# Attention and two feed-forward layers in one kernel: a new order of the first loads, six staging buffers, order edges for the weight decoding, and softmax sums in PSUM

## The chip, the cores and the metric

The kernel runs on one core of a Trainium2 chip. The metric is the device time of one launch in microseconds (us), from start to end, all inputs in HBM at the start and the output in HBM at the end. PE is the matrix engine, ACT, DVE and POOL are the three element-wise engines, SP is the queue from which all loads and stores are issued.

## The reference, cut to what matters

Inputs are q, k, v of 2 batches, 8 heads, 576 positions and 64 columns. Two attentions are added: a local one with a band mask, and one over positions averaged in groups of four, whose output is repeated four times. Its result is the x of a gated layer, and that layer's output the x of a layer of four experts.

```
def sm_attn(qq, kk, vv):          # softmax(qq kk^T / 8) vv
...
out_d = sm_attn(q_d, k_d, v_d)    # q_d, k_d, v_d: means over 4 positions
mask = np.abs(pos[:, None] - pos[None, :]) < 4
scores = np.where(mask, scale * q @ k^T, -1e9)
out_local = softmax(scores) @ v
x = np.repeat(out_d, 4, axis=2) + out_local      # then heads side by side: [1152, 512]
h = x @ w_in                                     # [512, 2048]
x = (h / (1 + np.exp(-h))) @ w_out               # [2048, 512]
for e in range(4):
    out += p[:, e:e + 1] * (np.maximum(x @ w1[e], 0) @ w2[e])
```

## The kernel before, in words

**Attention.** The work is cut into 16 jobs (class Job, `plan_jobs`, L470): a job is one batch, one pair of heads and one of two pieces of positions (256 or 320 queries, four or five blocks of 64). Its steps are put at ticks: `load_kq`, `load_vg`, `load_vw` (L251 to L280), `local_scores` (L345), `local_max`, `local_exp`, `local_sum` (L362 to L374), the pooled keys (`pool_kq_first` for jobs 0 to 3, L312, on PE, ACT and DVE; `pool_kq` on POOL for the rest), `down_scores` and `down_max` (L376, L388), `norm` (L396), `trans` (L405, L413 to L423), `values` (L432, L441 to L452) and `split_x` (L454), which writes the job's part of x as a rounded part xh (L457, ACT) and a rest xl (L458, DVE). Scores lie in PSUM tiles of a pool with two buffers (`s_p`), transposes and outputs in one each (`t_p`, `o_p`). The statistics of a job (maxima, sums, reciprocals) lie in a small SBUF tile `j.st`, in every second column.

**Weights.** The gated layer's weights come as 8 units of four pieces, s0 to s31, 512 KB each (`load_raw`, L173). Units 0 and 1 are the first half of `w_in`, units 2 and 3 the first half of `w_out`, units 4 to 7 the second halves. A piece lands in a staging buffer of the pool `stg` (three buffers) and is decoded by `split_raw` (L190): two ACT operations (L201, L202), one on DVE (L203), then the rounded part on ACT (L207) and the rest on POOL (L208). `split_piece` then loads the next piece (`load_piece`). The DVE operation of unit 1 is tied behind the last x of jobs 0 to 2, that of units 2 and 3 behind that of job 3 (`behind_job`); the ACT operations are tied to nothing.

**Products.** The gated layer runs over four chunks of positions (256, 320, 256, 320) and two halves. In the first chunk the first three column groups are started per job by `start_mm` (one piece of unit 0 and the x of one job each). `g1_step` makes h, `g1_evac` its gate (L540 to L547), `g2_step` the second product, whose sum for the first half goes to `acc` (L571). Every product is three matmuls of rounded parts and rests (`mm3`, L521). The experts follow (L664, L725, `outputs`).

**The order.** Each instruction has a priority (`prio`, `at_prio`), and the compiler's list scheduler orders every engine's queue by priority and its own estimate of when data are there; at run time each engine takes its queue strictly in order. `follow` adds an edge that fixes only an order. The names in `FIRST_LOADS` (L120) give the first loads their order on SP's queue. At L804 to L807 `LOAD_AT` and `SPLIT_AT` put the first calls of `load_piece` and `split_piece` at ticks. `shares` (L821) loads the expert shares `dpr`.

Of the kernel before, what the change touches and what calls it, by code (L numbers as in the profile page):

```python
# [42 lines left out]
LOAD_AT = (-27, -13, -10)  # L43
# [18 lines left out]
def attention_moe_kernel(ctx, tc, kqa, kqb, qtl, va, vb, w64, w1d, w2d, dpr, out):  # L62
# [57 lines left out]
    FIRST_LOADS = ("kq0", "kq1", "s0", "s1", "vg0", "vw0", "s2", "kq2", "vg1", "vw1", "s3", "kq3", "vg2", "vw2",  # L120
                   "vg3", "vw3", "s4", "s5", "s6", "kq4", "kq5")
# [25 lines left out]
    last_x = []  # L147
# [25 lines left out]
    def load_raw(u, j):  # L173
        if u < 8:
            t = stg_p.tile([128, 512], I64, tag="stg", name="stg64")
            load(f"s{4 * u + j}", t, w64[u, :, j * 512:(j + 1) * 512])
        else:
            t = stg_p.tile([128, 1024], F32, tag="stg", name="stg")
            o = (u - 8) * UW + j * 1024
            SP.dma_start(out=t, in_=w1d[0, :, o:o + 1024])  # L180
        loaded.append((u, j, t))

    def split_piece():
        u, j, t = loaded.popleft()
        with at_prio(needed(u, j) - LEAD_SPLIT):
            split_raw(u, j, t)
        held[0] -= 1
        load_piece()

    def split_raw(u, j, t):  # L190
        if j == 0:
            unit[u] = slot(u)
        h, l = unit[u]
        if u < 8:
            c = slice(j * 512, (j + 1) * 512)
            v = t.bitcast(I32).rearrange("p (n t) -> p n t", t=2)
            a = d_p.tile([128, 512], F32, tag="dec", name="dec")
            ai = a.bitcast(I32)

            top = t.bitcast(U16).rearrange("p (n t) -> p n t", t=4)[:, :, 1]  # L200
            ACT.activation(out=a, in_=v[:, :, 1].bitcast(F32), func=ACTF.Prelu, scale=2.0 ** -112, alpha=2.0 ** 32)  # L201
            ACT.activation(out=v[:, :, 0], in_=top, func=ACTF.Copy, scale=2.0 ** -13, bias=2.0 ** -14 - 0.5)  # L202
# [4 lines left out]
            ACT.activation(out=h[:, c], in_=a, func=ACTF.Copy)  # L207
            POOL.tensor_tensor(out=l[:, c], in0=a, in1=h[:, c].bitcast(F32), op=ALU.subtract)  # L208
# [54 lines left out]

    def load_vw(j):
        if j.i in (2, 3):
            j.vw = first_p.tile([72, 512], F32, name=f"vw_f{j.i}")
        else:
            j.vw = a2.tile([72, 640], F32, tag="vw", name="vw")
        if j.c == 0:
            load(f"vw{j.i}", j.vw[:, 0:512], va[j.b, j.hp, :, 1024:1536])  # L270
        else:
            SP.dma_start(out=j.vw, in_=vb[j.b, j.hp])

    def load_vg(j):
        if j.c == 0:
# [4 lines left out]
            load(f"vg{j.i}", j.vg, va[j.b, j.hp, :, 0:1024])  # L280
# [92 lines left out]
    def local_sum(j):  # L373
        DVE.tensor_reduce(out=j.st[:, 7:7 + j.nb], in_=j.lo, axis=AX.X, op=ALU.add)  # L374
# [6 lines left out]
    def tail_scores(l):  # L381
# [4 lines left out]
        l.st = a2.tile([128, 20, 2], F32, tag="st", name="st")[:, :, 0]  # L386

    def down_max(j):  # L388
# [65 lines left out]
    def split_x(j):  # L454
        n, hp = j.n, j.hp
        x0 = XOFF[2 * j.b + j.c]
        ACT.activation(out=xh[:, hp, x0:x0 + n], in_=j.xf[:, 0:n], func=ACTF.Copy)  # L457
# [3 lines left out]
        if j.i < 4:  # L461
            behind_job.update({1: i} if j.i < 3 else {2: i, 3: i})
# [358 lines left out]
    def shares():  # L821
        SP.dma_start(out=pr, in_=dpr)
# [169 lines left out]
```

## Time and profile before

| | us |
|---|---|
| three runs | 682.25, 689.22, 687.2 |
| their median | 687.2 |
| the profiled execution, device time | 688.92 |
| its span in the trace | 686.8 |

All times of the trace count from the start of the span. The profiled execution lies 1.7 us above the median; 2.1 us of its time lie around its span. Loads and stores are shown under SPq, where the time is that of issuing, not of the transfer. A row of the timeline merges neighbours of the same kind (x4: four of them) and ends with the idle time of its engine before it and what ended that.

### The profile page before, as it was taken

How to read it: one execution, taken by the hardware profiler on the slowest of the kernel's cores; microseconds unless marked ns; L12 is line 12 of the kernel's file. 1: busy time of each engine (PE TensorE's matmuls, PEld its weight loads, DVE VectorE, ACT ScalarE, POOL GpSimd, SP SyncE). 2: the span in 40 equal slices, each digit the busy share in tenths (PEclk: the TensorE clock that was granted, in tenths of full speed). 3: DMA queues.
4: the chain of work that ended last, by engine and by line, in shares of the span. 5: the costliest groups of instructions: out<-in, count | busy, mean ns of one | idle time of the engine just before them, and what ended most of it. 6: DMA issues, size and time to landing. Idle time of an engine off the chain costs nothing.

```text
span 686.8 us, 13770 instructions
## 1 busy us (share of the span) xinstructions
PE 654.2 (95%) x5516; PEld 637.2 (93%) x5516; DVE 422.4 (61%) x850; ACT 330.1 (48%) x753; POOL 244.2 (36%) x346
## 2 busy tenths in 40 slices
PE   5689879999999999999999999999999999999996
PEld 4568769998999999999999999999999999999995
DVE  3458957655534653675476875558854669755444
ACT  4459766557653642443335643346533355433321
POOL 4434851133330000552265433455422654332210
PEclk9999989999999999999999999999999999999998
DMA  8847652025130300050001320003210020000001
GB/s 235 283 128 228 186 163 71 22 63 185 62 123 2 114 10 1 5 191 20 1 1 63 124 61 2 1 18 107 93 31 1 1 63 1 1 31 23 11 32 46
DMA packets 16928, 48.17 MB, mean 70 GB/s; under 512 B 2976, under 2 KB 4256, under 8 KB 16864
## 3 DMA queue, kind: packets, MB, share of 16 engines
q1 hardware_dynamic: 16864, 47.29, 22.0%
q8 instruction: 43, 0.70, 0.4%
q14 instruction: 21, 0.17, 0.1%
HBM read 44.93 MB, written 2.36 MB: 69 GB/s over the span
## 4 chain that ended last, share of the span: by engine, by line
PE 85%; DMA 6%; DVE 4%; ACT 3%; issue 1%; SPq 0%; ACTq 0%; DVEq 0%
PE mm L521 54%; PE p L725 26%; DMA stg<-in_w_dram 6%; PE s L353 1%; DVE dec L203 1%; PE t L413 1%; ACT dec L201 1%; PE o L445 1%; PE o L441 1%; ACT stg L202 1%; DVE acc L753 1%; DVE gl L547 0%; DVE st L398 0%; PE s L377 0%; SPq L128 0%
## 5 line engine op out<-in xcount | busy, mean ns | idle before, releaser
L521 PE MATMUL mm<-xh,wbuf 128*128 128x256 f32 (+2 forms) x1280 | 266.2, 295 | 1.2 <-ACT xh L457 1.0
L521 PEld LDWEIGHTS mm<-xh,wbuf 128*128 128x128 f32 x1280 | 209.6, 189 | 1.7 <-ACT xh L457 1.3
L521 PE MATMUL mm<-xl,wbuf 128*128 128x256 f32 (+2 forms) x640 | 188.7, 295 | 0.0
L707 POOL TENSOR_TENSOR r<-r 128x128 f32<-128x128 f32 x160 | 93.4, 596 | 183.2 <-ACT r L701 143.8
L710 DVE TENSOR_TENSOR h<-r,h 128x384 fp32r<-128x384 f32 (+1 forms) x128 | 91.7, 719 | 64.6 <-ACT h L709 64.4
L521 PEld LDWEIGHTS mm<-xl,wbuf 128*128 128x128 f32 x640 | 120.7, 189 | 0.1
L709 ACT ACTIVATE h<-r 128x384 fp32r<-128x384 f32 (+1 forms) x128 | 73.2, 577 | 85.2 <-POOL r L707 54.1
L521 PE MATMUL mm<-gh,wbuf 128*128 128x256 f32 (+2 forms) x512 | 105.3, 299 | 3.6 <-DVE gf L541 2.0
L725 PE MATMUL p<-wext,h 128*128 128x256 f32 x672 | 91.5, 279 | 0.0
L521 PEld LDWEIGHTS mm<-gh,wbuf 128*128 128x128 f32 x512 | 83.7, 191 | 4.6 <-ACT acc L571 1.5
L725 PE MATMUL p<-wbuf,h 128*128 128x256 f32 x672 | 84.5, 278 | 0.0
L725 PEld LDWEIGHTS p<-wext,h 128*128 128x128 f32 x672 | 84.4, 188 | 0.0
L725 PEld LDWEIGHTS p<-wbuf,h 128*128 128x128 f32 x672 | 81.2, 188 | 0.0
L521 PE MATMUL mm<-gl,wbuf 128*128 128x256 f32 (+2 forms) x256 | 74.6, 297 | 0.0
L701 ACT ACTIVATE r<-mm 128x512 f32<-128x512 f32 x48 | 28.6, 597 | 75.9 <-PE mm L521 75.5
L707 DVE TENSOR_TENSOR r<-r 128x128 f32<-128x128 f32 x96 | 33.4, 349 | 37.7 <-ACT r L701 33.1
L547 DVE TENSOR_TENSOR gl<-gf,gh 128x256 fp32r<-128x256 f32 (+2 forms) x64 | 38.5, 609 | 17.6 <-ACT gh L546 16.6
L521 PEld LDWEIGHTS mm<-gl,wbuf 128*128 128x128 f32 x256 | 48.9, 191 | 0.1
L541 DVE SCALAR_TENSOR_TENSOR gf<-th,mm 128x256 f32<-128x256 f32 (+2 forms) x64 | 28.6, 450 | 24.6 <-ACT th L540 23.7
L208 POOL TENSOR_TENSOR wbuf<-dec,wbuf 128x512 fp32r<-128x512 f32 x24 | 32.5, 1363 | 28.5 <-DVE gf L541 14.2
L753 DVE SCALAR_TENSOR_TENSOR acc<-p,pr,acc 128x256 f32<-128x256 f32 (+1 forms) x63 | 36.1, 605 | 5.9 <-PE p L725 5.9
L652 POOL TENSOR_TENSOR wext<-kst,wext 128x512 fp32r<-128x512 f32 x8 | 10.7, 1343 | 78.8 <-ACT wext L650 44.6
(130 smaller groups left out, 946.8 us busy)
## 6 DMA issues: line engine op xcount, KB each, us to landing
stg<-in_w_dram SPq DMA_DIRECT2D x32, 512.0 KB
kst<-in_w2d_dram SPq DMA_DIRECT2D x16, 512.0 KB
kst<-in_w1d_dram SPq DMA_DIRECT2D x12, 512.0 KB
kq<-in_kqa_dram SPq DMA_DIRECT2D x7, 419.0 KB
kq<-in_kqb_dram SPq DMA_DIRECT2D x8, 323.0 KB
stg<-in_w1d_dram SPq DMA_DIRECT2D x4, 512.0 KB
vw<-in_vb_dram SPq DMA_DIRECT2D x8, 180.0 KB
out_dram<-acc SPq DMA_DIRECT2D x5, 256.0 KB
```

The costliest lines, as they stand in the source:

```text
L201: ACT.activation(out=a, in_=v[:, :, 1].bitcast(F32), func=ACTF.Prelu, scale=2.0 ** -112, alpha=2.0 ** 32)
L208: POOL.tensor_tensor(out=l[:, c], in0=a, in1=h[:, c].bitcast(F32), op=ALU.subtract)
L521: ins = [PE.matmul(out=ps, lhsT=l, rhs=r, start=(first and i == 0), stop=(last and i == n - 1)) for i, (l, r) in enumerate(pairs)]
L541: DVE.scalar_tensor_tensor(out=gf[:, 0:n], in0=th[:, 0:n], scalar=1.0, in1=ps[:, 0:n], op0=ALU.add, op1=ALU.mult)
L547: latest[DVE] = DVE.tensor_tensor(out=gl[ft][:, 0:n], in0=gf[:, 0:n], in1=gh[ft][:, 0:n].bitcast(F32), op=ALU.subtract)
L652: b = eng.tensor_tensor(out=l[:, r], in0=x, in1=h[:, r].bitcast(F32), op=ALU.subtract)
L701: ACT.activation(out=r[:, 0:4].rearrange("p s t -> p (s t)"), in_=ps[:, 0:512], func=ACTF.Relu)
L707: latest[eng] = eng.tensor_tensor(out=r[:, o], in0=r[:, a], in1=r[:, b], op=op)
L709: ACT.activation(out=h, in_=r[:, part], func=ACTF.Copy)
L710: latest[DVE] = DVE.tensor_tensor(out=l, in0=r[:, part], in1=h.bitcast(F32), op=ALU.subtract)
L725: ins = [PE.matmul(out=ps, lhsT=x, rhs=y, start=(opens and k == 0 and i == 0), stop=(k == 3 and i == n - 1), skip_group_check=True) for i, ...
L753: DVE.scalar_tensor_tensor(out=o, in0=ps, scalar=p, in1=o, op0=ALU.mult, op1=ALU.add)
```

## The change

The first loads have a new order: keys, queries and values of jobs 0 to 3, then the weights. Job 3's keys get a place in `acc`, which is unused until the first `g2_step`, in place of a shared buffer. Six pieces are requested before the first is decoded; of the first 16 pieces those with i % 6 > 2 lie in `acc`, the others in the three staging buffers. Pieces are decoded behind given operations by order edges: s0, s1 behind the normalization of job 0 and s2, s3 behind that of job 1 (both ACT operations behind its ACT scaling, the DVE operation behind its DVE product), s4, s5 behind the x of job 0, s6, s7 behind that of job 2, units 2 and 3 behind that of job 3. The loads for jobs 8 and 9 are tied behind the load of s13, and the load of the expert shares behind the last load of the attention. The sums of the two softmaxes go to unused columns of the job's score tile in PSUM, the statistics tile has one column beside the other.

```
-LOAD_AT = (-27, -13, -10)
+LOAD_AT = (-27, -13, -10, -10, -10, -10)
...
-    FIRST_LOADS = ("kq0", "kq1", "s0", "s1", "vg0", "vw0", "s2", "kq2", "vg1", "vw1", "s3", "kq3", "vg2", "vw2",
-                   "vg3", "vw3", "s4", "s5", "s6", "kq4", "kq5")
+    FIRST_LOADS = ("kq0", "kq1", "vg0", "vw0", "kq2", "vg1", "vw1", "kq3", "vg2", "vw2", "vg3", "vw3",
+                   "s0", "s1", "s2", "s3", "kq4", "s4", "s5", "kq5")
...
     def load_raw(u, j):
         if u < 8:
-            t = stg_p.tile([128, 512], I64, tag="stg", name="stg64")
-            load(f"s{4 * u + j}", t, w64[u, :, j * 512:(j + 1) * 512])
+            i = 4 * u + j
+            if i < 16 and i % 6 > 2:
+                o = 1024 * (i % 6 - 2)
+                t = acc[:, o:o + 1024].bitcast(I64)
+            else:
+                t = stg_p.tile([128, 512], I64, tag="stg", name="stg64")
+            piece_load.append(load(f"s{4 * u + j}", t, w64[u, :, j * 512:(j + 1) * 512]))
...
     def split_piece():
         u, j, t = loaded.popleft()
+        i = 4 * u + j
...
-        load_piece()
+        if i < 10 or 11 < i < 15 or i > 15:
+            load_piece()
...
-            if u in behind_job:
-                follow(i, behind_job[u], "first weights")
+            key = (u, j) if u < 2 else u
+            if key in behind_job:
+                for a in (first, low):
+                    follow(a, behind_job[key][0], "first weights")
+                follow(i, behind_job[key][1], "first weights")
...
     def load_kq(j):
         kw = S + 6 if j.c == 0 else CT[1] + 6
-        if j.i == 2:
+        if j.i == 3:
+            j.kq = acc[:, 0:kw + j.n]
+        elif j.i == 2:
...
+        elif j.i in (8, 9):
+            follow(i, piece_load[j.i + 5], "weights")
...
-        j.st = a2.tile([128, 20, 2], F32, tag="st", name="st")[:, :, 0]
+        j.st = a2.tile([128, 20], F32, tag="st", name="st")
...
-        DVE.tensor_reduce(out=j.st[:, 7:7 + j.nb], in_=j.lo, axis=AX.X, op=ALU.add)
+        DVE.tensor_reduce(out=j.ps[:, 496:496 + j.nb], in_=j.lo, axis=AX.X, op=ALU.add)
...
-                       accum_out=j.st[:, 7 + j.nb:8 + j.nb])
+                       accum_out=j.ps[:, 496 + j.nb:497 + j.nb])
...
     def norm(j):
         nb = j.nb
-        DVE.tensor_scalar(out=j.st[:, 7:8 + nb], in0=j.st[:, 7:8 + nb], scalar1=1e-9, scalar2=None, op0=ALU.add)
-        DVE.reciprocal(out=j.st[:, 13:14 + nb], in_=j.st[:, 7:8 + nb])
+        sums = j.ps[:, 496:497 + nb]
+        DVE.tensor_scalar(out=sums, in0=sums, scalar1=1e-9, scalar2=None, op0=ALU.add)
+        DVE.reciprocal(out=j.st[:, 13:14 + nb], in_=sums)
...
+        if nb and j.i < 2:
+            behind_job.update({(0, 2 * j.i): (a, i), (0, 2 * j.i + 1): (a, i)})
...
     def split_x(j):
...
-        if j.i < 4:
-            behind_job.update({1: i} if j.i < 3 else {2: i, 3: i})
+        for key in {0: ((1, 0), (1, 1)), 2: ((1, 2), (1, 3)), 3: (2, 3)}.get(j.i, ()):
+            behind_job[key] = (a, i)
...
     def shares():
-        SP.dma_start(out=pr, in_=dpr)
+        follow(SP.dma_start(out=pr, in_=dpr), last_load[-1], "shares")
```

## Rows read from the trace of the kernel before

**Rows 1.** The page: PE's busy share in 40 slices of the span, in tenths.

```profile
PE   5689879999999999999999999999999999999996
```

**Rows 2.** Windows: busy us (instructions) per engine, granted clock, DMA share, GB/s.

```profile
0.00:54.60 54.60, 36.52 (x319) 28.15 (x319) 26.42 (x70) 28.71 (x70) 23.38 (x43) 0.97 0.70 211
54.60:91.90 37.30, 33.58 (x404) 30.04 (x403) 33.87 (x73) 31.92 (x87) 27.41 (x38) 0.96 0.69 217
0.00:91.90 91.90, 70.09 (x721) 58.19 (x721) 60.29 (x143) 60.64 (x156) 50.79 (x80) 0.96 0.70 214
91.90:100.40 8.50, 5.81 (x48) 5.46 (x48) 4.24 (x12) 4.66 (x14) 4.17 (x9) 0.71 0.52 159
100.40:140.00 39.60, 39.60 (x447) 35.82 (x446) 24.22 (x70) 22.77 (x70) 4.08 (x12) 0.98 0.15 41
...
0.00:30.00 30.00, 17.10 (x119) 12.89 (x120) 12.26 (x31) 13.81 (x31) 15.73 (x30) 1.00 0.90 273
...
60.00:70.00 10.00, 10.00 (x116) 9.39 (x114) 9.21 (x24) 10.00 (x31) 4.45 (x6) 1.00 0.76 250
```

**Rows 3.** The chain that ended last, in order of time: start us, us, what.

```profile
3.52 10.76 DMA stg<-in_w_dram
...
16.01 8.42 DMA stg<-in_w_dram
...
161.60 147.31 PE mm L521 x1134
```

**Rows 4.** Timeline of ACT, from 14 to 35 us.

```profile
14.30 0.66 ACT L202 ACTIVATE stg<-stg 128x512 int32<-128x512 uint16 x1 [1.25 <-DMA stg<-in_w_dram]
14.86 0.39 ACT L371 ACTIVATE s<-s 128x280 f32<-128x280 f32 x1
...
34.17 0.39 ACT L371 ACTIVATE s<-s 128x280 f32<-128x280 f32 x1
34.84 0.66 ACT L202 ACTIVATE stg<-stg 128x512 int32<-128x512 uint16 x1 [0.28 <-DMA stg<-in_w_dram]
```

**Rows 5.** Timeline: the ends of jobs 2 and 3, and the last piece of unit 3.

```profile
44.20 0.41 DVE L458 TENSOR_TENSOR xl<-o,xh 128x256 fp32r<-128x256 f32 x1
...
54.16 0.42 DVE L458 TENSOR_TENSOR xl<-o,xh 128x256 fp32r<-128x256 f32 x1 [0.23 <-ACT xh L457]
...
90.60 1.28 POOL L208 TENSOR_TENSOR wbuf<-dec,wbuf 128x512 fp32r<-128x512 f32 x1
```

**Rows 6.** Timeline: first scores, job 0's subtraction and weights' product, job 3's keys issued.

```profile
4.08 2.20 PE L353 MATMUL s<-kq 64*64 64x70 f32 x32 [4.08 <-DMA kq<-in_kqa_dram]
...
7.50 0.46 DVE L367 TENSOR_TENSOR s<-s,st 128x280 f32<-128x280 f32 x1
...
18.34 0.37 SPq L128 DMA_DIRECT2D kq<-in_kqa_dram  x1
...
20.11 0.81 DVE L402 TENSOR_TENSOR sm<-s,st 128x280 f32<-128x280 f32 x2
```

**Rows 7.** Groups of ACT, 0 to 91.9 us: busy us, mean ns | idle before.

```profile
L202 ACT ACTIVATE stg<-stg 128x512 int32<-128x512 uint16 x19 | 12.7, 669 | 4.0 <-DMA stg<-in_w_dram 3.9
L201 ACT ACTIVATE dec<-stg 128x512 f32<-128x512 f32 x17 | 11.3, 667 | 11.3 <-DMA stg<-in_w_dram 11.2
L207 ACT ACTIVATE wbuf<-dec 128x512 fp32r<-128x512 f32 x16 | 10.0, 628 | 0.6 <-DVE dec L203 0.6
```

**Rows 8.** Groups of DVE, 0 to 91.9 us, adding 1e-9 to the sums, and the pooled maximum.

```profile
L398 DVE TENSOR_SCALAR st<-st 128x5 f32<-128x5 f32 (+2 forms) x11 | 5.6, 520 | 0.5 <-ACT ed L393 0.4
...
L391 DVE TENSOR_REDUCE st<-s 128x1 f32<-128x144 f32 x11 | 3.3, 299 | 2.5 <-PE s L377 2.5
```

**Rows 9.** Line 398 alone (min/median/max ns), and its longest with POOL's row beside it.

```profile
L398 DVE TENSOR_SCALAR st<-st x18: 154/169/2273, 19.3 to 131.0; 128x5 f32<-128x5 f32 x8, 128x6 f32<-128x6 f32 x8, 128x1 f32<-128x1 f32 x2
...
80.75 2.27 DVE L398 TENSOR_SCALAR st<-st 128x5 f32<-128x5 f32 x1
...
81.72 1.27 POOL L208 TENSOR_TENSOR wbuf<-dec,wbuf 128x512 fp32r<-128x512 f32 x1
```

More of the change, by code (lines that the diff above doesn't have):

```diff
@@ L196, in split_raw @@
             v = t.bitcast(I32).rearrange("p (n t) -> p n t", t=2)
-            a = d_p.tile([128, 512], F32, tag="dec", name="dec")
-            ai = a.bitcast(I32)
+            d = d_p.tile([128, 512], F32, tag="dec", name="dec")
+            ai = d.bitcast(I32)
             top = t.bitcast(U16).rearrange("p (n t) -> p n t", t=4)[:, :, 1]
-            ACT.activation(out=a, in_=v[:, :, 1].bitcast(F32), func=ACTF.Prelu, scale=2.0 ** -112, alpha=2.0 ** 32)
-            ACT.activation(out=v[:, :, 0], in_=top, func=ACTF.Copy, scale=2.0 ** -13, bias=2.0 ** -14 - 0.5)
+            first = ACT.activation(out=d, in_=v[:, :, 1].bitcast(F32), func=ACTF.Prelu, scale=2.0 ** -112, alpha=2.0 ** 32)
+            low = ACT.activation(out=v[:, :, 0], in_=top, func=ACTF.Copy, scale=2.0 ** -13, bias=2.0 ** -14 - 0.5)
             i = DVE.scalar_tensor_tensor(out=ai, in0=ai, scalar=3, in1=v[:, :, 0],
                                          op0=ALU.logical_shift_left, op1=ALU.bitwise_or)
-            if u in behind_job:
-                follow(i, behind_job[u], "first weights")
-            ACT.activation(out=h[:, c], in_=a, func=ACTF.Copy)
-            POOL.tensor_tensor(out=l[:, c], in0=a, in1=h[:, c].bitcast(F32), op=ALU.subtract)
+            key = (u, j) if u < 2 else u
[3 more added lines that the diff above has]
+                follow(i, behind_job[key][1], "first weights")
+            ACT.activation(out=h[:, c], in_=d, func=ACTF.Copy)
+            POOL.tensor_tensor(out=l[:, c], in0=d, in1=h[:, c].bitcast(F32), op=ALU.subtract)
         else:
@@ L279, in load_vg @@
                 j.vg = ac.tile([128, 256, 4], F32, tag="vg", name="vg")[0:72]
-            load(f"vg{j.i}", j.vg, va[j.b, j.hp, :, 0:1024])
+            i = load(f"vg{j.i}", j.vg, va[j.b, j.hp, :, 0:1024])
+            if j.i == 8:
+                follow(i, piece_load[13], "weights")
     def load_tail(l):
@@ L385, in tail_scores @@
                       rhs=kd[l.b, hp], start=True, stop=True, tile_position=(0, 32 * hp))
-        l.st = a2.tile([128, 20, 2], F32, tag="st", name="st")[:, :, 0]
+        l.st = a2.tile([128, 20], F32, tag="st", name="st")
     def down_max(j):
@@ L393, in down_max @@
         ACT.activation(out=j.ed, in_=pd, func=ACTF.Exp, scale=SC_D, bias=j.st[:, 6:7],
-                       accum_out=j.st[:, 7 + j.nb:8 + j.nb])
+                       accum_out=j.ps[:, 496 + j.nb:497 + j.nb])
     def norm(j):
         nb = j.nb
-        DVE.tensor_scalar(out=j.st[:, 7:8 + nb], in0=j.st[:, 7:8 + nb], scalar1=1e-9, scalar2=None, op0=ALU.add)
-        DVE.reciprocal(out=j.st[:, 13:14 + nb], in_=j.st[:, 7:8 + nb])
+        sums = j.ps[:, 496:497 + nb]
+        DVE.tensor_scalar(out=sums, in0=sums, scalar1=1e-9, scalar2=None, op0=ALU.add)
+        DVE.reciprocal(out=j.st[:, 13:14 + nb], in_=sums)
         if nb:
             j.sm = a2.tile([128, nb, WIN], F32, tag="sm", name="sm")
-            DVE.tensor_tensor(out=j.sm, in0=j.lo, in1=j.st[:, 13:13 + nb].unsqueeze(2).to_broadcast([128, nb, WIN]), op=ALU.mult)
-        ACT.activation(out=j.ed, in_=j.ed, func=ACTF.Copy, scale=j.st[:, 13 + nb:14 + nb])
+            i = DVE.tensor_tensor(out=j.sm, in0=j.lo, in1=j.st[:, 13:13 + nb].unsqueeze(2).to_broadcast([128, nb, WIN]), op=ALU.mult)
+        a = ACT.activation(out=j.ed, in_=j.ed, func=ACTF.Copy, scale=j.st[:, 13 + nb:14 + nb])
+        if nb and j.i < 2:
+            behind_job.update({(0, 2 * j.i): (a, i), (0, 2 * j.i + 1): (a, i)})
     def trans(j):
@@ L456, in split_x @@
         x0 = XOFF[2 * j.b + j.c]
-        ACT.activation(out=xh[:, hp, x0:x0 + n], in_=j.xf[:, 0:n], func=ACTF.Copy)
+        a = ACT.activation(out=xh[:, hp, x0:x0 + n], in_=j.xf[:, 0:n], func=ACTF.Copy)
         i = DVE.tensor_tensor(out=xl[:, hp, x0:x0 + n], in0=j.xf[:, 0:n], in1=xh[:, hp, x0:x0 + n].bitcast(F32),
```

4 lines of the change are left out of this document (2 added, 2 removed).

## The prediction

> **What bounds the kernel now.** I read the page first. PE is the engine to fill: from the seventh slice to the end nearly every slice shows 9, and only the first six, about 100 us, are loose [rows 1]. The windows say where it ends: from 100.4 to 140 us PE is busy all 39.6 us, from 91.9 to 100.4 only 5.8 of 8.5, at a granted clock of 0.71 [rows 2]. The chain of waits agrees: from 161.6 us it holds 1134 matmuls of one line in a row, while ahead of 40 us it runs through the landing of weight pieces, 10.8 and 8.4 us in one step [rows 3]. So what counts is the moment at which PE can go on without stopping. For that it needs the decoded units 2 and 3 of the weights, the last of which POOL finishes at 90.60 + 1.28 = 91.9 us [rows 5]. The rest up to 100.4 us is the end of the first chunk's second product.
>
> What sets 91.9 us? Two stretches behind one another. Up to 54.6 us, when job 3's x ends (54.16 + 0.42, [rows 5]), ACT is busy 28.7 us of 54.6 and DVE 26.4. From there to 91.9 us ACT is busy 31.9 of 37.3 (0.86) and DVE 33.9 (0.91) [rows 2]: here these two are the bound. In the first stretch they wait, and the ACT timeline shows for what: at 14.30 us ACT stands at a decode whose piece has just landed, and job 0's exponential, whose input was ready at 7.50 + 0.46 = 7.96 us [rows 6], runs only behind it, at 14.86. At 34.84 us ACT again starts a decode just as its piece lands [rows 4]. A queue in strict order is held by a transfer that the four jobs don't need. In the ACT groups, waits for pieces come to 11.2 + 3.9 = 15.1 us [rows 7]. Also, job 3's keys are only issued at 18.34 us [rows 6], since they share job 0's buffer.
>
> **The change part by part.**
>
> *Load order.* By the tile shapes keys and queries of a job among the first four have 0.43 MB, values 0.29 + 0.15 MB; four jobs 3.49 MB, a piece 0.52 MB. At the 273 GB/s of the first 30 us [rows 2] and some 2 us of latency (the first keys land at 4.08, [rows 6]), the four jobs' inputs are in at about 15 us, s0 at 16.7, s3 at 22.5, s7 (with the keys of jobs 4 and 5) at 32.6, and s15, with what jobs 4 to 7 need, 14.1 MB in all, at 53.5 us. So the pieces start about 9 us later than before, but four jobs no longer have to wait for keys.
>
> *Job 3's x without ACT being held.* From keys to a ready exponential job 0 took 4.08 to 7.96, 3.9 us [rows 6]; from job 2's exponential at 34.17 [rows 4] to the end of its x at 44.20 + 0.41 it took 10.4 us [rows 5]; together 14.3. Two score tiles go round, and job 0's comes free with the product that followed its exponential by 20.11 − 14.86 = 5.3 us [rows 6, 4]: from 7.96 that is 13.3 us. Job 2 then ends at 27.6, job 3, behind it through the one output tile, some 3 us later: about 30 us. I don't believe in no hold at all. The decodes of s0 to s3 are placed behind the normalizations, but may still stand in ACT's queue ahead of copies of jobs 0 and 1. Each piece costs ACT 0.669 + 0.667 + 0.628 = 1.96 us [rows 7], four cost 7.9. I add them whole: job 3's x at 38 us; bounds 30 and 44.
>
> *The two ACT edges and the DVE edge per piece* are orders, with no work. Behind a held decode stand all later ACT operations, jobs and gates alike. From row to row this can cost nothing (30 us above) or as much as now (the second rival).
>
> *Six buffers.* They add no transfer. Before, a piece could be requested only when one of three was decoded. I price them by what they allow: s15 in at 53.5 us instead of after 74, so that units 2 and 3 are bound by engines, not landings. Alone they are worth nothing while ACT is full, and at most the 4.0 us of L202's waits [rows 7].
>
> *The rest of the work.* To 91.9 us ACT does 60.6 us of work [rows 2]. At job 3's x it had done 28.7, with eight pieces nearly decoded; with four less 28.7 − 7.9 = 20.8. At 38 us I take 23 as done. The other 37.6 at the 0.86 of the second stretch take 43.7 us: 38 + 43.7 = 81.7 us. For DVE 60.3 − 23 = 37.3 at 0.91 take 41.0: 79. ACT is later and decides: 91.9 becomes 81.7, a gain of 10.2 us.
>
> *Sums in PSUM.* L398 takes 0.52 us in the mean over the first 91.9 us [rows 8] against a median of 0.169, and 2.27 at its longest, which ends just as POOL's 1.27 us beside it do [rows 9]. If it no longer has to wait, DVE has 11 x (0.52 − 0.17) = 3.9 us less work. The bound from the other side: the wait passes to the next DVE operation, nothing gained. As ACT is later than DVE by 2.7 us, I count nothing. [...]
>
> Against it: the sums now cost PSUM accesses. The row nearest is L391, which reads 144 PSUM values in 0.299 us [rows 8], against L398's 0.17 for five in SBUF; I take nothing more, with 0.13 us (the whole difference) times 3 operations times 9 jobs = 3.5 us as the upper bound. [...] No row here has a PSUM operation this small.
>
> *The edges on loads.* The load of the shares leaves SP's queue early; nothing waits for it. Those of jobs 8 and 9 wait for s13; their x is not wanted before the second chunk's products are through, and from 100.4 to 140 us DVE is busy 24.2 and ACT 22.8 of 39.6 us [rows 2]. That slack also says why the gain isn't lost later: behind the first chunk only PE is full, and all of it starts 10.2 us earlier.
>
> **Sum.** The profiled execution becomes 688.9 − 10.2 = 678.7 us; it lies 1.7 us above the median of the runs, so I forecast 687.2 − 10.2 = 677.0. With job 3's x at 30 us and 20.8 done: 30 + 39.8 / 0.86 = 76.3, gain 15.6: 671.6. At 44 us and 25 done: 85.4, gain 6.5: 680.7. These are its own range.
>
> **Rivals.**
> [...]
>
> *Second, no change: ACT is held as before, only by other pieces.* The scheduler only estimates landings: at 14.30 us its order had cost an exponential ready at 7.96 over 6 us. If s7 stands ahead of job 3's copies, landing at 32.6, job 3's x follows as it did behind 34.84, 54.6 − 34.8 = 19.8 us later, at 52.4; then the second stretch as it was, 37.3: 89.7, gain 2.2, 685.0 us. For it: nothing else tells the scheduler more about DMA. Against: s6 and s7 are behind the x of job 2.
>
> *Third, slower: the weights pay for the inputs.* The same hold, with transfers at the 211 GB/s of the first stretch [rows 2]: s7 needs 8.3 MB, lands at 41.5, job 3's x is at 61.3, the pieces are free at 98.6, 6.7 us later: 693.9 us; a piece more and it is 696. It decides from the point at which job 3's x comes later than 54.6 us. Against: 273 GB/s in the first 30 us.
>
> That the edges change nothing, because the queue already had that order, is the second rival with its price.
>
> **How the numbers follow.** Forecast 0.54, first rival 0.16, second 0.21, third 0.09. About 1% (6.9 us) is what a measurement of this kernel can tell from no change. Faster by more: the forecast's own range, the first rival, none of the second: 0.70. Slower by more: the later part of the third, 0.06. Within: 0.24. The range reaches from 667 (the first rival) to 688, beyond the second rival by the 3 us of a PSUM price or a longer hold; outside are half of the third rival and what beats the first.
>
> **What would show it.** Right: job 0's exponential near 8 us, job 3's x between 30 and 44 us, the last rest of unit 3 by POOL at 76 to 86 us, PE without stops from about 90 us, L398 never over 0.3 us. Wrong: ACT idle before decodes for landings in sum as long as now, job 3's x after 50 us, or PE stopping between 100 and 165 us for x of later jobs or for unit 4.

## The result, and the profile after

The changed kernel takes 678.29 us (median of 4 runs, 676.94 to 679.52), the kernel before 685.35 us beside it (4 runs, 682.25 to 689.22): a ratio of 0.9898 with a 95% interval of 0.986 to 0.9937. The forecast was 677.0 us in a range of 667 to 688. The two profiled executions stand further apart, 688.92 and 679.06 us, 9.9 us, because that of before was one of its longest. Twelve later runs of the changed kernel gave 679.45 us against 685.06, a ratio of 0.9906 (0.987 to 0.9941). By the two ratios the gain is 6 to 7 us.

The page, PE's and the DMA engines' busy share in 40 slices of the span:

```profile
PE   4879999999999999999999999999999999999995
...
DMA  8964612116501200140003310013300020000001
```

The loose slices at the start are three; in [rows 1] they were six. The windows of the changed kernel (columns as in [rows 2]), up to job 3's x, from there to the last rest of unit 3, the first half of the gated layer, and what is behind it:

```profile
0.00:43.40 43.40, 31.10 (x308) 24.88 (x312) 24.92 (x68) 26.92 (x67) 22.93 (x43) 0.96 0.83 276
43.40:75.00 31.60, 27.80 (x293) 25.04 (x293) 25.40 (x58) 28.12 (x74) 19.89 (x22) 0.89 0.61 195
...
0.00:188.80 188.80, 170.83 (x1682) 155.22 (x1683) 116.71 (x276) 127.98 (x325) 82.12 (x116) 0.97 0.50 159
188.80:677.10 488.30, 481.38 (x3837) 481.18 (x3835) 301.86 (x574) 202.63 (x429) 163.01 (x230) 1.00 0.12 37
```

The same two stretches of the kernel before, PE alone (busy, clock, DMA share, GB/s):

```profile
0.00:201.80 201.80, 175.80 (x1682) 0.97 0.48 149
201.80:686.80 485.00, 478.36 (x3836) 1.00 0.12 37
```

The first half ends 13.0 us earlier (201.8 to 188.8) with the same 1682 matmuls: PE stands idle for 18.0 us in it instead of 26.0, and its busy time is 5.0 us shorter (170.83 for 175.80; what shortens it is not shown). Behind it 3.3 us are lost again (485.0 to 488.3 us); experiment 5 deals with those. So the gain is made in the first half, and a part of it seems to be given back.

The ACT timeline of the changed kernel, in place of [rows 4]: job 0's exponential and the first decode.

```profile
8.20 1.28 ACT L336 ACT_TABLE_LOAD   x1 [8.20 <-DVE s L383]
10.60 0.29 ACT L336 ACTIVATE kd<-s 128x144 f32<-128x144 f32 x1 [1.12 <-PE s L333]
10.93 0.39 ACT L387 ACTIVATE s<-s 128x280 f32<-128x280 f32 x1
...
17.33 0.67 ACT L208 ACTIVATE dec<-stg 128x512 f32<-128x512 f32 x1 [0.18 <-DMA stg<-in_w_dram]
```

No decode stands ahead of the exponential any more, which goes from 14.86 to 10.93 us. It is not at 8: a table load of 1.28 us and a copy that waits for PE now stand there. The ends of job 3's x, and the last rest of unit 3 (DVE and POOL timelines), which answer to [rows 5]:

```profile
43.00 0.41 DVE L477 TENSOR_TENSOR xl<-o,xh 128x256 fp32r<-128x256 f32 x1
...
73.73 1.29 POOL L218 TENSOR_TENSOR wbuf<-dec,wbuf 128x512 fp32r<-128x512 f32 x1
```

54.6 us became 43.4, and 91.9 became 75.0. The groups of ACT up to 75 us show that it no longer stands waiting for pieces; in [rows 7] these waits were 15.1 us, here 0.9 + 0.2 + 0.2:

```profile
L209 ACT ACTIVATE stg<-stg 128x512 int32<-128x512 uint16 x12 | 8.1, 686 | 0.9 <-DMA stg<-in_w_dram 0.9
L208 ACT ACTIVATE dec<-stg 128x512 f32<-128x512 f32 x10 | 6.6, 673 | 0.8 <-POOL wbuf L218 0.5 <-DMA stg<-in_w_dram 0.2
L208 ACT ACTIVATE dec<-acc 128x512 f32<-128x512 f32 x7 | 4.8, 686 | 0.3 <-POOL wbuf L218 0.3
L209 ACT ACTIVATE acc<-acc 128x512 int32<-128x512 uint16 x7 | 4.7, 687 | 0.2 <-DMA acc<-in_w_dram 0.2
```

And the sums, now in PSUM, line by line (min/median/max ns), in place of [rows 9]:

```profile
L415 DVE TENSOR_SCALAR s<-s x18: 158/170/172, 15.9 to 134.9; 128x5 f32<-128x5 f32 x8, 128x6 f32<-128x6 f32 x8, 128x1 f32<-128x1 f32 x2
```

### The profile page after: what moved, and what is told of

Read it like the earlier page. It is cut to its first block, busy times and chain, and to the rows that moved or that the text cites. A ratio compares the mean times of both kernels' runs of the same rounds, so it can differ in the third digit from the quotient of the medians.

```text
span 677.1 us, 13739 instructions
## 1 busy us (share of the span) xinstructions
PE 652.2 (96%) x5516; PEld 636.4 (94%) x5516; DVE 418.6 (62%) x850; ACT 330.6 (49%) x753; POOL 245.1 (36%) x346
## 4 chain that ended last, share of the span: by engine, by line
PE 82%; DMA 5%; ACT 4%; DVE 4%; POOL 3%; issue 1%; SPq 0%; ACTq 0%; POOLq 0%
PE mm L540 53%; PE p L744 26%; DMA stg<-in_w_dram 3%; DVE dec L210 1%; DMA vg_f<-in_va_dram 1%; ACT dec L208 1%; PE s L369 1%; DMA vg<-in_va_dram 1%; POOL wbuf L218 1%; POOL kq L306 1%; PE t L432 1%; DVE acc L772 1%; PE o L464 1%; ACT wbuf L217 0%; ACT stg L209 0%
## 5 line engine op out<-in xcount | busy, mean ns | idle before, releaser
L540 PE MATMUL mm<-xh,wbuf 128*128 128x256 f32 (+2 forms) x1280 | 269.4, 297 | 5.5 <-DVE gf L560 3.6
L540 PE MATMUL mm<-gh,wbuf 128*128 128x256 f32 (+2 forms) x512 | 103.5, 296 | 1.0 <-DVE gf L560 0.9
L540 PEld LDWEIGHTS mm<-gh,wbuf 128*128 128x128 f32 x512 | 82.3, 188 | 1.5 <-DVE gf L560 1.1
L720 ACT ACTIVATE r<-mm 128x512 f32<-128x512 f32 x48 | 28.7, 597 | 76.1 <-PE mm L540 75.7
L726 DVE TENSOR_TENSOR r<-r 128x128 f32<-128x128 f32 x96 | 33.6, 351 | 37.6 <-ACT r L720 33.0
L566 DVE TENSOR_TENSOR gl<-gf,gh 128x256 fp32r<-128x256 f32 (+2 forms) x64 | 37.6, 589 | 18.9 <-ACT gh L565 18.1
L671 POOL TENSOR_TENSOR wext<-kst,wext 128x512 fp32r<-128x512 f32 x8 | 10.7, 1342 | 79.9 <-ACT wext L669 44.3
```

The source lines that it names most:

```text
L540: ins = [PE.matmul(out=ps, lhsT=l, rhs=r, start=(first and i == 0), stop=(last and i == n - 1)) for i, (l, r) in enumerate(pairs)]
L566: latest[DVE] = DVE.tensor_tensor(out=gl[ft][:, 0:n], in0=gf[:, 0:n], in1=gh[ft][:, 0:n].bitcast(F32), op=ALU.subtract)
L671: b = eng.tensor_tensor(out=l[:, r], in0=x, in1=h[:, r].bitcast(F32), op=ALU.subtract)
L720: ACT.activation(out=r[:, 0:4].rearrange("p s t -> p (s t)"), in_=ps[:, 0:512], func=ACTF.Relu)
L726: latest[eng] = eng.tensor_tensor(out=r[:, o], in0=r[:, a], in1=r[:, b], op=op)
```

## The experiments

Theory: four parts (order, edges, buffers, ties of the loads) do one job together, which is to have pieces landed and ACT free at the same time. The rival is that one of them carries the gain and the others are worth what the prediction gave them, nothing. So each part was undone alone, and one was done alone. In the table "profiled" is the device time of the one profiled execution of each kernel, and the columns behind it are read from that execution, in us: the issue of the load of s15, the end of job 3's x, the last rest of unit 3, the time between these two, the end of the first half. The last two rows belong to experiment 5.

| kernel | median us | ratio to before (95%) | profiled | s15 issued | job 3's x | unit 3 | x to unit 3 | first half |
|---|---|---|---|---|---|---|---|---|
| before | 685.35 | | 688.92 | 74.3 | 54.6 | 91.9 | 37.3 | 201.8 |
| before, again | 685.76 | 0.9989 (0.9968 to 1.001) | 685.75 | 72.3 | 52.3 | 90.3 | 38.0 | 198.7 |
| changed | 678.29 | 0.9898 (0.986 to 0.9937) | 679.06 | 48.1 | 43.4 | 75.0 | 31.6 | 188.8 |
| changed, again | 679.45 | 0.9906 (0.987 to 0.9941) | 675.26 | 48.6 | 43.8 | 74.0 | 30.2 | 187.9 |
| old load order | 680.81 | 0.9924 (0.9893 to 0.9955) | 685.15 | 55.7 | 51.0 | 82.0 | 31.0 | 195.6 |
| old edges | 688.53 | 1.0032 (1.0007 to 1.0057) | 684.83 | 58.1 | 46.0 | 85.9 | 39.9 | 197.5 |
| no edges on ACT | 680.54 | 0.9925 (0.99 to 0.9949) | 680.07 | 47.4 | 44.4 | 75.7 | 31.3 | 191.9 |
| three buffers, no ties | 684.41 | 0.9985 (0.9952 to 1.0019) | 684.42 | 63.6 | 45.4 | 79.6 | 34.2 | 195.0 |
| three buffers | 684.21 | 0.9989 (0.9954 to 1.0025) | 686.11 | 64.5 | 47.7 | 80.2 | 32.5 | 197.0 |
| no ties of jobs 8, 9 | 685.19 | 1.0005 (0.9977 to 1.0033) | 686.90 | 51.2 | 46.2 | 82.4 | 36.2 | 198.9 |
| before + new edges | 691.75 | 1.0065 (1.0035 to 1.0096) | 692.33 | 71.1 | 53.7 | 90.1 | 36.4 | 205.2 |
| sums in SBUF | 681.68 | 0.9954 (0.9907 to 1.0001) | 681.68 | 51.0 | 46.3 | 75.7 | 29.4 | 194.6 |
| one matmul more | 675.57 | 0.9862 (0.9826 to 0.9898) | 675.49 | 49.0 | 44.3 | 73.6 | 29.3 | 187.2 |
| one matmul more, again | 677.87 | 0.9876 (0.983 to 0.9923) | 681.26 | 52.9 | 48.2 | 79.3 | 31.1 | 193.7 |

A profiled execution is a single one, up to 4.3 us away from the median of its kernel (old load order). The last two rows are the changed kernel instruction by instruction up to the end of the first half, and still these columns lie 4 to 6.5 us apart. So the medians say what a part is worth, and an entry of the columns says something only where it goes beyond such a spread. The time from job 3's x to the last rest is steadier: 29.3 to 31.6 us in the four profiles with the changed first half, 37.3 and 38.0 in the two of before. The old load order, the missing ACT edges and the sums in SBUF leave it there (31.0, 31.3, 29.4); three buffers make it 32.5 and 34.2, missing ties 36.2, the old edges 39.9.

An edit also does more than it says: the scheduler gives the engines' queues another order. Instruction by instruction up to 185 us of the profiles, ACT's queue differs from the changed kernel's at 13 of 313 places with the old load order, but at 163 of 317 with the sums in SBUF, at 206 of 308 without the ties, and at 226 to 271 of 311 to 320 with three buffers (and ties), the old edges or no ACT edges. So the price of an undone part is that of the part together with such a new order; no run separates the two.

**1. The yardstick.** The kernel before, unedited, in the middle of the others.

> The kernel before once more, for the stretch of the second half's first product (471 matmuls, 53.2 us before and 55.2 us after the change). If the rate of 256-column matmuls (113 or 118 ns from start to start) belongs to a run or a chip, this profile may show 55 us, and the time of the same program moves by 2 to 3 us. If it belongs to the program's order, it shows 53.2 us again. Time 682 to 689 us.

A ratio of 0.9989: the two profiled executions differ by 3.1 us in the first half and by nothing behind it (485.0 us both times; the 256-column matmuls go at 113 ns again). Differences of a median below about 2 us are left undecided here.

**2. Load order and edges.** Undone alone in the changed kernel; first the order:

```
-    FIRST_LOADS = ("kq0", "kq1", "vg0", "vw0", "kq2", "vg1", "vw1", "kq3", "vg2", "vw2", "vg3", "vw3",
-                   "s0", "s1", "s2", "s3", "kq4", "s4", "s5", "kq5")
+    FIRST_LOADS = ("kq0", "kq1", "s0", "s1", "vg0", "vw0", "s2", "kq2", "vg1", "vw1", "s3", "kq3", "vg2", "vw2",
+                   "vg3", "vw3", "s4", "s5", "s6", "kq4", "kq5")
```

> The changed kernel with the old order of the first loads; job 3's keys stay in their own place, six buffers, edges and sums stay. Held-queue theory (the gain comes from jobs 0 to 3 not standing behind pieces): the edges keep the decodes behind the normalizations, but keys and values land later, job 2's keys at 17 us instead of 13; x of job 3 moves from 43.4 to 46 to 50 us and 3 to 5 us of the gain go: 681 to 683 us. Rival, the buffers: the pieces come sooner than in the changed kernel, the time stays within 2 us of it.

0.9924: the new order by itself is worth 0.0018 to 0.0026 of the time against the two measurements of the changed kernel, 1 to 2 us, within their intervals; the 3 to 5 us of the held-queue theory were not lost. Job 3's x comes at 51.0 us instead of 43.4, though in an execution 4.3 us above the median, and the stretch behind it is as long as in the changed kernel (31.0 us).

Then the edges as they were (one per unit, on DVE alone):

```
-            key = (u, j) if u < 2 else u
-            if key in behind_job:
-                for a in (first, low):
-                    follow(a, behind_job[key][0], "first weights")
-                follow(i, behind_job[key][1], "first weights")
+            if u in behind_job:
+                follow(i, behind_job[u], "first weights")
...
-        for key in {0: ((1, 0), (1, 1)), 2: ((1, 2), (1, 3)), 3: (2, 3)}.get(j.i, ()):
-            behind_job[key] = (a, i)
+        if j.i < 4:
+            behind_job.update({1: i} if j.i < 3 else {2: i, 3: i})
```

> The changed kernel with the decoding tied as before: only the DVE operation of units 1 to 3 behind the last x of the jobs, no edge on ACT. Held-queue theory: ACT stands at s0 again while job 0's exponential is ready, from 9 to 17 us; x of job 3 comes after 46 us and the time loses 3 to 6 us. Rival: with the inputs first the queue has that order anyway, and the time stays within 2 us.

1.0032: all of the gain and 2 us more are gone, with the new order, the six buffers, the ties and the PSUM sums all in place. Job 3's x is nearly where it was (46.0), but s4 and s5 are done at 45.5 and 46.8 us instead of 33.2 and 34.4: in the old rule all of unit 1 waits on DVE for job 2, so the buffers of s4 to s7 stay full, s10 is requested at 43.5 us instead of 30.2, and s15 at 58.1 instead of 48.1. Job 0's exponential stands at 11.24 us, against 10.93. So by this execution it is when the buffers come free, and not the exponentials, that the edges decide.

Then only the edges on ACT taken out, the one on DVE kept for each piece:

```
-                for a in (first, low):
-                    follow(a, behind_job[key][0], "first weights")
```

> The changed kernel with the new edges on the DVE operation of each piece alone, none on the two ACT operations. In the kernel with the old edges s4 and s5 were decoded only behind the x of job 2 (their rests ended at 45.5 and 46.8 us against 33.2 and 34.4 in the changed one), so its loss can come from the late DVE edge as well as from a free ACT. Held-queue theory (ACT edges matter): 684 to 689 us. Rival (the piece-wise DVE edges matter, ACT follows by itself): within 2 us of the changed kernel, 676 to 681 us.

0.9925, s15 requested at 47.4 us, last rest at 75.7. By the medians the ACT edges are worth some 2 us or less, within the intervals; what counts is the finer edge on DVE.

Last, the edges alone, put into the kernel before (order, three buffers and sums of before):

```
+        if nb and j.i < 2:
+            behind_job.update({(0, 2 * j.i): (a, i), (0, 2 * j.i + 1): (a, i)})
...
+                for x in (first, low):
+                    follow(x, behind_job[key][0], "first weights")
+                follow(i, behind_job[key][1], "first weights")
```

> The kernel before with the edges alone: each decode's three operations behind the given operations of the jobs, piece by piece; old load order, three buffers, sums in SBUF. Theory (the parts need one another: with the old load order the pieces land first and hold three buffers, and the edges alone only hold them longer): no gain, ratio 0.995 to 1.005, job 0's exponential earlier than 14.86 us, but the last rest of unit 3 still at 86 to 92 us. Rival (the edges carry the change by themselves, since taking them out of the changed kernel gave back all of its gain): ratio 0.988 to 0.993 and last rest by 82 us.

1.0065, so 4.5 us slower than before (the medians, 691.75 and 685.06, lie 6.7 us apart). The groups of ACT, 0 to 90.1 us, look cured:

```profile
L202 ACT ACTIVATE stg<-stg 128x512 int32<-128x512 uint16 x19 | 12.6, 677 | 2.8 <-DMA stg<-in_w_dram 2.6
L201 ACT ACTIVATE dec<-stg 128x512 f32<-128x512 f32 x17 | 11.2, 665 | 2.2 <-POOL wbuf L211 2.2
```

The waits for pieces have fallen from 15.1 us [rows 7] to 2.6, and the kernel is slower. SP's queue (issue times) has a stretch from 36.9 to 50.7 us without a request for a piece:

```profile
36.91 0.33 SPq L129 DMA_DIRECT2D stg<-in_w_dram  x1
...
50.67 13.13 SPq L129 DMA_DIRECT2D stg<-in_w_dram  x5
```

But that is not where it loses. The kernel before has a longer one, from 26.5 (the second of the two) to 45.3 us:

```profile
23.51 3.34 SPq L128 DMA_DIRECT2D stg<-in_w_dram  x2
...
45.28 0.93 SPq L129 DMA_DIRECT2D stg<-in_w_dram  x2
```

And s15 and the last rest come even a little earlier here than in the kernel before (71.1 and 90.1 us for 74.3 and 91.9). The loss lies behind the last rest. PE's windows from there to the end of the first half, here and in the kernel before:

```profile
90.10:205.20 115.10, 109.96 (x1039) 0.99 0.32 99
...
91.90:201.80 109.90, 105.71 (x962) 0.97 0.31 94
```

The weights are ready, but 1039 matmuls of the first half are still to be done instead of 962: other work was pushed back. By then ACT had rounded x for seven jobs, in the kernel before for eight.

So the rival fell. Without the edges the buffers gain nothing (1.0032), without the buffers the edges gain nothing (0.9989, experiment 3). No run has the six buffers alone in the kernel before.

**3. Buffers and ties.** Three staging buffers, as before:

```
-LOAD_AT = (-27, -13, -10, -10, -10, -10)
+LOAD_AT = (-27, -13, -10)
...
-            if i < 16 and i % 6 > 2:
-                o = 1024 * (i % 6 - 2)
-                t = acc[:, o:o + 1024].bitcast(I64)
...
-        if i < 10 or 11 < i < 15 or i > 15:
-            load_piece()
+        load_piece()
```

In the first such run the ties of the loads of jobs 8 and 9 were left out too; the second has them.

> The changed kernel with three staging buffers (no pieces in the accumulator, three requests ahead, the two ties behind s13 left out since they have no place then). Held-queue theory: the first jobs keep their times, x of job 3 within 2 us of 43.4, but the pieces of units 2 and 3 come one by one; the last rest of unit 3 goes from 75.0 to 80 to 85 us and the time loses 3 to 6 us. If the buffers carry the whole gain: the last rest near 91.9 us, 685 us or more. If they carry nothing: within 2 us of the changed kernel.

> The changed kernel with three staging buffers again, but with the loads of jobs 8 and 9 still behind pieces s13 and s14 (the earlier run with three buffers had lost these ties too). Theory (buffers and ties do one job together: the pieces must be requested ahead of inputs that nobody wants yet; each alone is not enough): the pieces again wait for a free buffer, the last rest of unit 3 comes at 79 to 84 us instead of 75, and 3 to 6 us of the gain are lost: 681 to 684 us, ratio to before 0.994 to 0.998. Rival (in the earlier run only the missing ties counted, the three further buffers are worth nothing): last rest at 74 to 77 us, ratio 0.988 to 0.992, as the changed kernel.

684.41 and 684.21 us, 0.9985 and 0.9989: 5 to 6 us of the gain are lost both times. In the second, on the same chip as the changed kernel's 679.45 us, it is 4.8 us by the medians. The rival, that only the missing ties had counted, fell. SP's queue of the second:

```profile
21.58 7.16 SPq L128 DMA_DIRECT2D stg<-in_w_dram  x3
...
45.42 11.99 SPq L129 DMA_DIRECT2D stg<-in_w_dram  x5
```

And that of the changed kernel:

```profile
19.30 6.20 SPq L129 DMA_DIRECT2D stg<-in_w_dram  x3
...
40.80 0.93 SPq L129 DMA_DIRECT2D stg<-in_w_dram  x2
41.78 0.42 SPq L129 DMA_DIRECT2D kq<-in_kqa_dram  x1
...
48.14 0.33 SPq L129 DMA_DIRECT2D acc<-in_w_dram  x1
```

With six buffers s15 is requested at 48.1 us, with three at 64.5, and job 8's keys directly behind s13 in both. Of these 16 us little reaches the last rest: from job 3's x to it 32.5 us instead of 31.6 and 30.2.

Then six buffers without the ties:

```
-        elif j.i in (8, 9):
-            follow(i, piece_load[j.i + 5], "weights")
...
-            if j.i == 8:
-                follow(i, piece_load[13], "weights")
```

> The changed kernel without the ties of the loads for jobs 8 and 9 behind s13. Job 8's values are on the chain of waits at 81 to 87 us there. If these ties cost: POOL no longer waits at 81 to 87 us, x of job 8 before 90 us, 1 to 3 us gained. If they protect the pieces: s13 to s15 land later, the last rest of unit 3 after 77 us, 1 to 3 us lost.

1.0005: nothing is left of the gain. SP's queue of this kernel:

```profile
19.09 1.58 SPq L129 DMA_DIRECT2D kq<-in_kqa_dram  x2
21.62 4.28 SPq L129 DMA_DIRECT2D stg<-in_w_dram  x3
...
28.72 0.32 SPq L129 DMA_DIRECT2D vg<-in_va_dram  x1
```

More keys (x2) go ahead of the pieces at 19.09 us; the values follow at 28.72. s15 is then 3.1 us later, as is job 3's x (2.8). That is less than half of the 7.4 us by which the last rest is late. A part of the rest is lost between 66 and 70 us, as this timeline of POOL, DVE, ACT and PE shows:

```profile
66.44 1.04 POOL L302 TENSOR_TENSOR vg<-vg 72x512 f32<-72x512 f32 x1 [2.30 <-DMA vg<-in_va_dram]
...
66.91 3.07 DVE L562 TENSOR_TENSOR gl<-gf,gh 128x256 fp32r<-128x256 f32 x1
67.44 1.26 POOL L218 TENSOR_TENSOR wbuf<-dec,wbuf 128x512 fp32r<-128x512 f32 x1
68.66 1.04 POOL L302 TENSOR_TENSOR kq<-kq 128x288 f32<-128x288 f32 x2
...
70.35 0.42 ACT L561 ACTIVATE gh<-gf 128x256 fp32r<-128x256 f32 x1 [3.21 <-DVE gf L556]
...
70.37 0.39 PE L536 MATMUL mm<-gh,wbuf 128*128 128x256 f32 x1 [1.84 <-DVE gf L556]
...
71.42 0.38 DVE L562 TENSOR_TENSOR gl<-gf,gh 128x256 fp32r<-128x256 f32 x1
```

A DVE operation that takes 0.38 us at 71.42 takes 3.07 here, and ends 0.3 us behind the last of three POOL rows that follow one another; ACT waits 3.2 us behind it and PE 1.8. In the changed kernel this operation (L566, 256 columns) took 0.41 to 0.43 us in the 32 cases with no POOL operation beside it and 0.65 to 1.51 us in the eight others, and each of these eight ended some 0.3 us behind the end of a POOL operation, as in these two rows:

```profile
61.54 1.09 POOL L306 TENSOR_TENSOR vd<-vg 72x256 f32<-72x256 f32 x1
...
62.05 0.87 DVE L566 TENSOR_TENSOR gl<-gf,gh 128x256 fp32r<-128x256 f32 x1
```

So here a part of the cost is where POOL's work comes to lie, not the transfer. This is one profiled execution; how much of the 7 us it is in the others stays open.

**4. The sums back in SBUF.** `st` in every second column and the sums in it, as before:

```
-        sums = j.ps[:, 496:497 + nb]
+        sums = j.st[:, 7:8 + nb]
```

> The changed kernel with the sums in SBUF as before. L398's counterpart takes 6.9 us in 18 before and 3.0 after the change. If DVE is the bound between 45 and 85 us, 3 to 4 us are lost: 681 to 683 us, and single additions of 1 to 2 us are back. If ACT or the landings are: the additions are as long, and the time stays within 2 us of the changed kernel.

0.9954 against 0.9898 and 0.9906, 3 to 4 us, with intervals that overlap. Its longest addition took 0.64 us, not 2.27:

```profile
L415 DVE TENSOR_SCALAR st<-st x18: 154/170/639, 16.4 to 132.8; 128x5 f32<-128x5 f32 x8, 128x6 f32<-128x6 f32 x8, 128x1 f32<-128x1 f32 x2
```

All 18 additions together took 4.0 us here and 3.0 in the changed kernel, as these groups show, so they can't be the 3 us by themselves:

```profile
L415 DVE TENSOR_SCALAR st<-st 128x5 f32<-128x5 f32 (+2 forms) x18 | 4.0, 223 | 2.0 <-ACT ed L409 1.7
...
L415 DVE TENSOR_SCALAR s<-s 128x5 f32<-128x5 f32 (+2 forms) x18 | 3.0, 168 | 1.8 <-ACT ed L409 1.5
```

The last rest comes at 75.7 us as in the changed kernel. The sign is likely, but the path of these 3 us is not shown; the new order of the queues is a rival that no run rules out.

**5. The loss behind the first half.** The first 471 matmuls behind the first half, in the kernel before (window, PE busy, clock, DMA):

```profile
202.77:256.00 53.23, 53.23 (x471) 1.00 0.13 41
```

The same 471 in the changed kernel:

```profile
189.80:244.99 55.19, 55.19 (x471) 1.00 0.13 39
```

PE is full and its granted clock 1.00 in both, yet the same work takes 2.0 us longer: 256-column matmuls start 113 ns apart in the one and 118 in the other. Two theories: the level belongs to the program, or it is drawn anew in each run. First one matmul more, to shift all that follow, then the changed kernel itself and the same edit once more beside it:

```
+            if u0 == 4 and o == 0 and ft == 0 and k == 0:
+                l, r = g1_pairs(u0, ft, k, c)[0]
+                PE.matmul(out=ps[:, 0:n], lhsT=l, rhs=r, start=True, stop=True)
```

> The changed kernel with one matmul more: the first of the second half of the gated layer is done twice. Behind the first half the kernel before needs 99.4 us to the last rounded part of the second half, the changed one 102.1, with the same matmuls at 113 and at 118 ns from start to start. If that level depends on a position in PE's stream (odd or even), one matmul more brings 99.4 us and a time 2 to 3 us below the changed kernel; if on something set long before, 102.2 us and the same time.

> The changed kernel once more, as the measure for the next run beside it: ratio to before 0.986 to 0.994; last rest of unit 3 at 75 us, and 256-column matmuls from 200 us on at 118 ns from start to start, if that level belongs to the program.

> The kernel with the first matmul of the second half done twice, once more, beside the changed kernel on the same chip. Theory (the level of 113 or 118 ns belongs to the program and is worth what it says): 332 matmuls at 113 instead of 118 ns, 1.7 us faster than the changed kernel, give or take the 0.1 us of the added matmul and the spread of the first 200 us. Rival (the 2.7 us seen were the spread between runs): no difference, ratio to the changed kernel within 0.2% of 1.

In the first run of the edit some 240 matmuls went at 118 ns and the other 256-column ones, some 330, at 113, and it took 675.57 us (0.9862, 0.9826 to 0.9898), the lowest median here. But the unedited changed kernel then ran the same stretch at the faster level from the first matmul on:

```profile
188.87:242.10 53.23, 53.23 (x471) 1.00 0.12 41
```

So the theory that the level belongs to the program fell. The edited kernel beside it took 677.87 us (0.9876, 0.983 to 0.9923) against 679.45 (0.9906, 0.987 to 0.9941): its intervals overlap the changed kernel's, and it isn't shown to be faster. With the faster level the stretch behind the first half takes 485.3 us (673.2 less 187.9), as in the kernel before. So the 3.3 us come and go with the run; the program alone does not bring them. Whether the change makes the slower level more frequent stays open: it is in none of the three profiles of the kernel before and its edit, and in seven of the eleven of the changed kernel and its edits, in six of them for a part of the stretch only.

## Why the prediction was right, and which of its steps were not

**What bounded the kernel** was read rightly in one half: the moment at which PE can go on, and the gain was made in the stretch where it was looked for. The other half, that the time is lost by ACT standing at decodes whose pieces have not landed, is not borne out. Up to the last rest these waits came to 15.1 us in the kernel before and to 0.7 to 6.0 us in every edited kernel of experiments 2 to 4, in those of 680 us (0.7 with the old order, 5.7 without ACT edges) as in those of 684 to 692 us (2.3 without ties, 2.6 with the edges alone). Taking these waits away is not enough to make the kernel faster. The waits of ACT (us in total, times, longest) without ties up to 82.4 us, and without ACT edges up to 75.7:

```profile
ACT stg L209 <- DMA stg<-in_w_dram: 1.8, 2, 1.1
ACT dec L208 <- DMA stg<-in_w_dram: 0.3, 1, 0.3
ACT acc L209 <- DMA acc<-in_w_dram: 0.2, 1, 0.2
...
ACT stg L209 <- DMA stg<-in_w_dram: 3.6, 2, 1.8
ACT dec L208 <- DMA stg<-in_w_dram: 2.1, 1, 2.1
```

**Job 3's x** came at 43.4 us, forecast 38, bounds 30 and 44. Two terms were too small. The exponential came at 10.9 and not 8, as the table load and a copy waiting for PE took the place of the decode; and seven pieces had been finished by 43.4 us, where the sum had put four ahead of it.

**The last rest of unit 3** came at 75.0 us, forecast 81.7, one us outside its stretch of 76 to 86. The density was nearly right (28.12 / 31.6 = 0.89 for 0.86). The term that failed is the work: 60.6 − 23 = 37.6 us were carried over whole from the kernel before, and ACT did 28.1. By then it had worked for 26.9 + 28.1 = 55.0 us instead of 60.6, since it had rounded x (xh) for jobs 0 to 5 only, and before for jobs 0 to 7. Two jobs had been pushed behind the weights. "Work to be done before this point" is not a constant when an edge reorders it.

**"All of it starts 10.2 us earlier"** failed as an argument. The last rest is 16.9 us earlier, the first half's end 13.0, the end of the profiled span 9.7 and the medians 6 to 7. The step took PE's work behind the last rest as given. But work had been pushed behind the weights, and PE had more left to do; from the last rest to the end of the first half it took 113.8 us in the changed kernel, against 109.9 (the window of before stands in experiment 2):

```profile
75.00:188.80 113.80, 111.93 (x1088) 1.00 0.34 104
```

1088 matmuls were left instead of 962, which takes back 3.9 us. Another 3.3 us were the slower matmuls of one run. And the profiled execution of before was 3.6 us above its median, where the prediction reckoned with 1.7, because a fourth run brought the median from 687.2 down to 685.35.

**Luck.** The time was met to 1.3 us, 678.29 for 677.0, but the gain was 7.1 us by these medians (5.6 by the later ones) where 10.2 were forecast; the lower median of before covers 1.9 us of the difference. And the 10.2 us came from two misses of opposite sign, too much work before the last rest and too little behind it, that cancelled in part.

**Six buffers** "alone are worth nothing while ACT is full, and at most 4.0 us": undone they cost 5 to 6 us, 4.8 on the same chip, a little over the bound. The step priced ACT's waits for landings, and those are 2.3 and 4.0 us with three buffers; pieces are requested 16 us later, and how that becomes the 5 us is shown only in part (1 to 4 us between job 3's x and the last rest).

**The edges** "can cost nothing or as much as now": undone they cost all the gain, and alone they made the kernel before 4.5 us slower. That they are orders with no work in them is right and says nothing of their price.

**The ties of loads** were counted at nothing, because nobody waits for those loads. This is the largest mistake: without them the gain is gone. The question was not who waits for the moved loads but who stands behind them in SP's queue, and, as far as one profile shows, what their arrival starts on POOL. How much of it is the new order of the queues is not shown.

**The sums in PSUM**: L398, never over 0.3 us, was right (2.27 became 0.17 us). That the wait goes with the sums in PSUM was an assumption; the traces agree with it. In the kernel before five of the 18 additions took 0.43 to 2.27 us, and each of the five ended 26 to 37 ns behind the end of a POOL operation; the other 13 took 0.154 to 0.174 us. In the changed kernel nine of the 18 lie beside a POOL operation and took 0.158 to 0.172 us, as the other nine did (0.164 to 0.172). One pair of rows from before, and one from the changed kernel:

```profile
49.67 1.27 POOL L208 TENSOR_TENSOR wbuf<-dec,wbuf 128x512 fp32r<-128x512 f32 x1
...
50.03 0.94 DVE L398 TENSOR_SCALAR st<-st 128x6 f32<-128x6 f32 x1
...
65.94 1.30 POOL L218 TENSOR_TENSOR wbuf<-dec,wbuf 128x512 fp32r<-128x512 f32 x1 [1.29 <-ACT wbuf L217]
...
66.81 0.17 DVE L415 TENSOR_SCALAR s<-s 128x6 f32<-128x6 f32 x1
```

With the sums back in SBUF one addition took 0.64 us (experiment 4). What holds such an addition there is not shown. The median is 170 ns in PSUM and 169 in SBUF [rows 9], so the bound of 3.5 us for PSUM accesses held with nothing in it. But the benefit was counted at nothing, because ACT decides, and experiment 4 makes it 3 us, if uncertainly.

**The rivals.** The first sets the lower end of the range, 667 us. Its terms were a DVE that POOL never holds and engines busy 0.94 of the time from job 3's x to the last rest, both the author's estimates. No run shows either: in the changed kernel ACT was busy 0.89 and DVE 0.80 (25.40 of 31.6 us) of that stretch, and six operations of L566 that lay beside one of POOL took 5.3 us in place of some 2.5. It had the weights nearly right (72.3 us at the last rest) and the end wrong, for the reason above. The second's hold was not seen: no decode waited long. But its price is what the kernel pays when edges, buffers or ties are missing: 684 to 688 us. The third was not seen in the changed kernel.

The losses of the four parts and the sums, each undone alone, add up to about 2 + 9 + 5 + 7 + 3 = 26 us, for a gain of 7. They are not shares of it.

## What to carry to other kernels

When an in-order engine waits for landings, look at the whole ring: when a load is requested, what holds its buffer, what lies ahead of it in the issuing queue, and which edge frees it. A wait that is gone is not time that is gained: the edges alone took the waits for pieces from 15.1 to 2.6 us and made the kernel slower, because they pushed back work that PE then still had to do. Count what is left behind the point that you bring forward. And price a load that is moved out of the way by what is queued behind it, not by who needs it.

## What the runs showed of the hardware

**Two levels of matmul spacing at one granted clock.** 256-column matmuls start 113 or 118 ns apart, over hundreds in a row, with PE full and the clock 1.00. The level differs between runs of one program. Of the fourteen profiles here seven have 113 ns throughout, one 118 throughout, and in six the level changes, from 118 to 113 or from 113 to 118, always at the same place of the program: about 240 matmuls into the second half, where the first product of its second chunk goes over from unit 4 to unit 5. Behind the first half the seven take 485.0 to 485.5 us, the one 488.3, and the six 486.0 to 486.3 or 487.1 to 487.4. What sets it stays open; it is worth 2 us for 471 matmuls.

**The rate of the first transfers differs from run to run.** The window from 10 to 20 us of the changed kernel's second profiled execution, which took 675.26 us:

```profile
10.00:20.00 10.00, 6.41 (x40) 5.10 (x39) 5.50 (x18) 5.56 (x15) 4.95 (x6) 0.80 1.01 340
```

And that of the kernel with one matmul more beside it, which took 681.26 us:

```profile
10.00:20.00 10.00, 6.06 (x24) 5.41 (x25) 4.64 (x17) 3.80 (x10) 3.34 (x4) 0.92 0.96 220
```

The DMA engines are about as busy in both (1.01 and 0.96), and move 340 and 220 GB/s. ACT's first decode in the one and in the other:

```profile
17.08 0.68 ACT L208 ACTIVATE dec<-stg 128x512 f32<-128x512 f32 x1
...
22.19 0.66 ACT L208 ACTIVATE dec<-stg 128x512 f32<-128x512 f32 x1 [3.03 <-DMA stg<-in_w_dram]
```

The first half ends at 187.9 and 193.7 us, and the rest takes 485.3 and 485.5: 5 of the 6 us between these two runs are there at the first decode. What makes the rate differ stays open. Where a change lies in that stretch, as here, one profiled execution says little of a few microseconds.
